# One stream of 53 mixed transfers in place of one key and one value transfer per head, in a decode step with a long cache

## The chip, the cores and the metric

The kernel runs on one core of one Trainium2 chip. Its time is the device time of one execution in microseconds. Before the change three runs gave 1057.06, 1057.39 and 1058.13 us; the median is 1057.39 us. All tensors are float32.

## The reference

One token passes through a block with modulation, attention over a cache of 8192 positions, and a small dense layer.

```python
mod = (_silu(c) @ w_mod)                       # 640 -> 6 x 640: sa, ca, ga, sb, cb, gb
h = _layernorm(x) * (1 + ca) + sa
# attention, 32 heads of 192, 8192 positions, one query
q = (h @ wq).reshape(32, 192)
p = softmax(q @ k_cache.T * 192 ** -0.5)       # per head
x = x + ga * ((p @ v_cache) @ wo)
h = _layernorm(x) * (1 + cb) + sb
r = relu(h @ w1 + b1) ** 2                     # 640 -> 1536
x = x + gb * (r @ w2 + b2)                     # 1536 -> 640
```

The two caches are 201 MB each; with the weights the kernel reads 451.8 MB and writes 2560 bytes.

## The kernel before, in words

**Layout.** A head's keys are one tile of 128 partitions x 64 positions x 192 numbers (6.29 MB), its values another of the same size, in an order that suits the value matmuls. Keys of 30 of the 32 heads carry a piece of weights behind them: behind an even head's keys the `wq` columns of the next pair of heads, behind an odd head's the `wo` rows of the pair before (0.98 MB). All these tiles share three buffers of one size (`slot`, line 54). A load waits until the buffer's last readers are done. All loads go out on SyncE's queue, in program order: first `wm0` (the first two modulation vectors' weights, the first query weights and all small vectors), then K and V of each head in turn, then the remaining weights.

**Per head.** `keys` (line 192) takes the tile in two halves of 32 positions: VectorE multiplies all 32 x 192 products by the query in place (line 201), GpSimd adds the two halves of the rows of the last 14 positions (203), and VectorE sums the rows of the first 18 (204) and the halved rows of the last 14 (205). `softmax` (216) takes the maximum over positions on each partition, then over the partitions through a matmul with the identity and a row maximum (218 to 222), and ScalarE takes the exponential, four copies of each (228), with the sum of each row beside it. `values` (233) multiplies the probabilities with the value tile on PE, 24 products of 512 columns per head, three side by side in strips of 32 rows of the result (240). A float32 product is two instructions on PE, so 48 per head.

**Per pair of heads.** One head later `project` (245) divides by the sums and picks the diagonal of the two heads' results on VectorE (lines 254 and 256), and turns the rows into columns through a matmul (258). `attend` (260) multiplies them with `wo`, summing in one PSUM bank over all pairs. `query` (177) makes the two queries of the next pair.

**The end.** The last head's keys come in four pieces. The `wm1` weights come before and behind the last values: the last pair's `wo` rows with the gate of the attention first, then the shift and scale of the second norm. Then come `w1` in two pieces with the last gate's weights (`gb`) behind, and `w2` in five pieces of 6, 3, 1, 1 and 1 blocks. `gather` (275) spreads the sums over the partitions, `layernorm` (100) follows, then the product with `w1` (343), the square of the positive part, the last gate's product (351), some products whose result nothing reads (355), and the product with `w2` (363). The output goes out at line 368.

**Order.** The program fixes the order of instructions on each engine itself; nothing reorders them. Each engine works through its own list and waits for other engines through semaphores.

## Time and profile before

| | |
|---|---|
| median of three runs | 1057.39 us |
| the profiled execution: span | 1055.5 us |
| data moved by SyncE's queue | 451.83 MB |
| mean rate over the span | 428 GB/s |
| VectorE busy | 831.4 us |
| PE busy (matmuls) | 463.7 us |
| GpSimd busy | 194.8 us |
| ScalarE busy | 33.4 us |
| median time to landing, K with weights (7104 KB) | 27.4 us |
| median time to landing, V (6144 KB) | 22.1 us |

The span reaches from the first to the last instruction of the profiled execution; 1.9 us lie between it and the median of the runs, which are timed without a profile. A row such as `DVE k L201 <- DMA k<-in_kw: 134.4, 28, 7.5` says that line 201 on VectorE (DVE) stood idle for 134.4 us in total, 28 times, 7.5 us at the longest, until a transfer into a key tile had landed. PEld is the weight load of PE, SPq SyncE's queue. In a row of a timeline stand the start, the duration, the engine, the line, the operation, what it writes and reads, the shapes, and how many there are; in brackets the idle time before it. In a row of stretches stand the stretch, its length, the busy us of PE, PEld, DVE, ACT and POOL with their instructions, the granted PE clock, the DMA engines' busy share and their rate.

### The profile page before, as it was taken

Reading aid. Unit: us, or ns where it says so; the run is one execution under the profiler, and the core shown is the slowest. Engines: PE = TensorE matmul, PEld = TensorE weight load, DVE = VectorE, ACT = ScalarE, POOL = GpSimd, SP = SyncE. Lnnn points to the kernel's source line nnn. Section 1 sums busy time; section 2 is a strip of 40 time slices with the busy share of each in tenths; the row PEclk is TensorE's granted clock in tenths of the full one; section 3 lists DMA queues with packets and bytes.
Section 4 is the critical chain, followed back from the end, with each engine's and each line's share of the span. In section 5 each row is a group of like instructions: output and inputs, shape, how many; then the busy total and the mean of one; then the engine's idle time right before and its main releaser. Section 6 shows DMA issues by size and latency. Waiting matters only on the chain.

```text
span 1055.5 us, 5687 instructions
## 1 busy us (share of the span) xinstructions
PE 463.7 (44%) x2356; PEld 155.0 (15%) x2356; DVE 831.4 (79%) x409; ACT 33.4 (3%) x88; POOL 194.8 (18%) x72
## 2 busy tenths in 40 slices
PE   3234443355543345463334534335453335535446
PEld 1101111111111111120111111101111111111113
DVE  2886878978787987878888687997878798789963
ACT  1000000000000000000000000000000000000000
POOL 0211112211212221212221212221221221122110
PEclk9667666766666766666676666666666666767769
DMA  9999999999999999999999999999999999999997
GB/s 403 435 434 428 432 440 427 441 424 437 433 433 428 440 424 441 424 439 427 431 437 437 422 442 430 428 439 426 439 429 433 428 438 433 434 427 432 424 426 310
DMA packets 11410, 452.18 MB, mean 428 GB/s; under 512 B 1269, under 2 KB 1273, under 8 KB 1785
## 3 DMA queue, kind: packets, MB, share of 16 engines
q1 hardware_dynamic: 11384, 451.83, 99.3%
q8 instruction: 18, 0.29, 0.1%
q14 instruction: 8, 0.06, 0.0%
HBM read 451.82 MB, written 0.00 MB: 428 GB/s over the span
## 4 chain that ended last, share of the span: by engine, by line
DMA 42%; DVE 39%; PE 17%; ACT 1%; issue 1%; SPq 0%; DVEq 0%; ACTq 0%
DMA k<-in_kw 36%; DVE k L201 21%; PE ps_o L240 14%; DVE sc L204 12%; DVE sc L205 5%; DMA k<-in_ky 3%; DMA w_t<-in_w 2%; PE ps_mx L220 1%; DMA wm_t<-in_wm 1%; ACT p L228 1%; PE ps_sum L97 1%; PE ps_mod L140 1%; PE ps_q L181 1%; DVE nm L222 0%; DVE mp L218 0%
## 5 line engine op out<-in xcount | busy, mean ns | idle before, releaser
L201 DVE TENSOR_TENSOR k<-k,qb 128x6144 f32<-128x6144 f32 (+1 forms) x66 | 419.7, 6359 | 141.6 <-DMA k<-in_kw 134.4
L203 POOL TENSOR_TENSOR k<-k 128x1344 f32<-128x1344 f32 (+1 forms) x66 | 194.1, 2941 | 820.9 <-DVE k L201 476.1
L240 PE MATMUL ps_o<-v,p 128*32 128x512 f32 x1536 | 290.4, 731 | 17.2 <-ACT p L228 17.2
L204 DVE TENSOR_REDUCE sc<-k 128x18 f32<-128x3456 f32 (+1 forms) x66 | 240.5, 3644 | 4.3
L220 PE MATMUL ps_mx<-ident,mp 128*128 128x128 f32 x64 | 25.5, 501 | 416.2 <-DVE mp L218 416.2
L240 PEld LDWEIGHTS ps_o<-v,p 128*32 128x32 f32 x1536 | 68.4, 131 | 215.4 <-issue 193.1
L267 PE MATMUL att_a<-k,oT 128*32 128x320 f32 x180 | 49.6, 720 | 114.2 <-DVE oT L262 113.1
L205 DVE TENSOR_REDUCE sc<-k 128x14 f32<-128x1344 f32 (+1 forms) x66 | 99.0, 1500 | 0.0
L220 PEld LDWEIGHTS ps_mx<-ident,mp 128*128 128x128 f32 x64 | 16.1, 312 | 442.8 <-DVE mp L218 421.0
L181 PE MATMUL ps_q<-k,hR 128*128 128x384 f32 x150 | 52.3, 496 | 0.0
L228 ACT ACTIVATE p<-sc,nm 128x256 f32<-128x256 f32 x32 | 16.2, 508 | 760.6 <-DVE nm L222 496.9
L267 PEld LDWEIGHTS att_a<-k,oT 128*32 128x32 f32 x180 | 13.7, 161 | 136.7 <-DVE oT L262 116.7
L222 DVE TENSOR_REDUCE nm<-ps_mx 128x1 f32<-128x128 f32 x32 | 9.3, 291 | 28.5 <-PE ps_mx L220 28.5
L181 PEld LDWEIGHTS ps_q<-k,hR 128*128 128x128 f32 x150 | 27.3, 190 | 27.9 <-issue 11.7
L254 DVE SCALAR_TENSOR_TENSOR om<-ps_o,r,mask 96x512 f32<-96x512 f32 x32 | 23.9, 747 | 6.5 <-PE ps_o L240 5.4
L256 DVE TENSOR_REDUCE os<-om 96x64 f32<-96x512 f32 x32 | 21.8, 682 | 1.1
L140 PE MATMUL ps_mod<-wm_t,silu 128*32 128x320 f32 (+1 forms) x120 | 11.7, 550 | 14.6 <-DVE silu L128 14.6
L97 PE MATMUL ps_sum<-sp,ones 128*128 128x2 f32 x32 | 9.4, 364 | 17.2 <-ACT p L228 17.2
L183 ACT ACTIVATE qb<-ps_q 128x384 f32<-128x384 f32 x16 | 7.9, 491 | 195.2 <-PE ps_q L181 195.2
L97 PEld LDWEIGHTS ps_sum<-sp,ones 128*128 128x128 f32 x32 | 8.0, 312 | 21.9 <-ACT p L228 21.9
L145 DVE COPY mods<-ps_mod 128x320 f32<-128x320 f32 (+1 forms) x4 | 1.6, 398 | 10.2 <-PE ps_mod L140 10.2
L76 DVE COPY small<-wm_t 128x27 f32<-128x27 f32 x1 | 0.2, 179 | 11.2 <-DMA wm_t<-in_wm 11.2
(77 smaller groups left out, 90.9 us busy)
## 6 DMA issues: line engine op xcount, KB each, us to landing
k<-in_kw SPq DMA_DIRECT2D x29, 7104.0 KB, 27.4
v<-in_vc SPq DMA_DIRECT2D x32, 6144.0 KB, 22.1
k<-in_ky SPq DMA_DIRECT2D x1, 6144.0 KB, 28.3
k<-in_ky SPq DMA_DIRECT2D x2, 3072.0 KB, 21.5
k<-in_kw SPq DMA_DIRECT2D x3, 1536.0 KB, 15.5
wm_t<-in_wm SPq DMA_DIRECT2D x1, 4173.5 KB, 12.7
wm_t<-in_wm SPq DMA_DIRECT2D x1, 3200.0 KB, 29.3
wm_t<-in_wm SPq DMA_DIRECT2D x1, 2560.0 KB, 18.2
```

Of the source, the lines that this page charges most:

```text
L97: nc.tensor.matmul(ps[:, :n], ones, src, start=True, stop=True)
L140: nc.tensor.matmul(ps[32 * g:32 * (g + 1), :n * DG], e[:, b:b + 1].to_broadcast([P, 32]), wb[:, :, DG * g:DG * (g + 1)], start=(b == 0), s ...
L181: nc.tensor.matmul(ps[:, :PW], hR[:, b], w[:, b], start=(b == 0), stop=(b == KB - 1))
L201: nc.vector.tensor_mul(pr, pr, q[:, None, :].to_broadcast([P, n, DH]))
L203: nc.gpsimd.tensor_add(half, half, pr[:, m:, DH // 2:])
L204: nc.vector.tensor_reduce(s[:, :m], pr[:, :m], axis=AX.X, op=ALU.add)
L205: nc.vector.tensor_reduce(s[:, m:], half, axis=AX.X, op=ALU.add)
L220: nc.tensor.matmul(ps[:, :P], mp.to_broadcast([P, P]), ident, start=True, stop=True)
L228: nc.scalar.activation(p, sc[:, :, None].to_broadcast([P, NPOS, 32 // E]), AF.Exp, bias=nm, accum_out=sp[:, h % 2:h % 2 + 1])
L240: nc.tensor.matmul(ps_t[h][32 * g:32 * (g + 1)], p[:, E * j:E * (j + 1)].rearrange("p e r -> p (e r)"), t[:, j, g], start=(j == 0), stop=( ...
L254: nc.vector.scalar_tensor_tensor(om[:n], ps_t.pop(h)[:n].rearrange("p (d e) -> p d e", e=E), r2[:n, a:a + 1], mask[:n, None, :].to_broadca ...
L267: nc.tensor.matmul(att_a[32 * g:32 * (g + 1), :2 * DG], oT[:, 32 * j:32 * (j + 1)], w[:, j, 2 * DG * g:2 * DG * (g + 1)], start=(i == 0 an ...
```

## The change

K and V are no longer loaded head by head. The whole work is laid out as one array in the order of use and cut into 53 chunks, most of them 84 x 192 columns wide (8.26 MB), again in three buffers. A function `plan` writes down for each chunk how many key positions (of 128 x 192 numbers) and how many value units (8 positions each) it holds, and which piece of weights stands behind them.

- The first chunk is the whole first head's keys. Then most chunks hold 44 key positions and 5 value units; with a `wo` piece (0.98 MB) 34, with a `wq` piece (now 512 columns of `wq`, 1.31 MB, 12 pieces in place of 16) 30, with both 20 or 28. Keys end 40 to 84 positions ahead of the values after each of the chunks up to position 1300; from there on chunks hold a unit of values less until the keys are some 120 positions ahead. So the last two chunks hold values alone (and one `wo` piece). The last chunk is loaded in two pieces.
- Chunk n+3 is asked for at the end of the work on chunk n. Behind the chunks come `wm1` (2 pieces), a tile with the last gate's weights ahead of `w1` (2 pieces: the gate with three blocks, then two blocks) and `w2` (3 pieces of 8, 3 and 1 blocks).
- In each chunk come first the query product, then the values whose probabilities are there, the multiplication of all key positions (split where the head changes), GpSimd's half sums over the last 7/16, the evictions of heads that ended in the chunk before, the row sums, and, where a head's keys end, its maximum and exponential. Values that needed that softmax follow it, then the attention product with `wo`.
- Queries and scores live in rings (`qb`, `sc`) in place of a tile per pair or head; the probabilities get two buffers in place of one.
- The eviction picks the diagonal per head without the division; the division is on the three columns after the turn. Turns and maxima go through a transposing product in place of a product with the identity. The sums over partitions are formed from a copy on ScalarE, a transposing product and a row sum. `attend` puts the first 512 of the 640 outputs on one strip of the result and the rest on the three others.
- At the end the three modulation vectors of `wm1` are one product with `gather` after its third block; the last gate (`gate`) runs ahead of `w1`'s product in two halves of 64 rows, with its result copied by ScalarE; one product over the whole array takes the place of the eight on strips whose result nothing reads.

```diff
-W1_CUT = ((0, 3), (3, 2))
-W2_CUT = ((0, 6), (6, 3), (9, 1), (10, 1), (11, 1))
-WARM = 2
+QC = 512
+NQ = H * DH // QC
+RING = 3 * QC
+SRING = 4 * NPOS
+WQ = KB * QC
+UNIT = E * DH
+SLOT = 84 * DH
+VPC = 5
+LEAD_FROM = 1300
+LEAD = 120
+W1_CUT = (KB * D + 3 * FF, KB * D + KB * FF)
+W2_CUT = (8 * D, 11 * D, 12 * D)
+WM_CUT = (WO + 9 * D, WO + 15 * D)
+WARM = 1
...
+def plan():
+
+    chunks, kp, vp, q, o = [], 0, 0, 1, 0
+    while kp < H * NPOS or vp < H * NPOS // E:
+        room, w = SLOT, []
+        if o < NPAIR - 1 and 2 * (o + 1) * NPOS // E <= vp:
+            w.append(("o", o))
+            o, room = o + 1, room - WO
+        used = (QC * (q - 2) - 1) // DH + 1 if q > 2 else 0
+        if q < NQ and kp >= NPOS * (QC * q // DH) - 3 * NPOS // 2 and kp >= NPOS * used:
+            w.append(("q", q))
+            q, room = q + 1, room - WQ
+        if not chunks:
+            nk, nv = NPOS, 0
+        else:
+            v = VPC - 1 if kp >= LEAD_FROM else VPC
+            nk = min(H * NPOS - kp, (room - v * UNIT) // DH)
+            if kp + nk - E * (vp + v) > LEAD:
+                v += 1
+                nk = min(H * NPOS - kp, (room - v * UNIT) // DH)
+            nv = min(H * NPOS // E - vp, (room - nk * DH) // UNIT)
+            while nv and ((vp + nv - 1) // (NPOS // E) + 1) * NPOS > kp + nk:
+                nv -= 1
+            nk = min(H * NPOS - kp, (room - nv * UNIT) // DH)
+        chunks.append((kp, nk, vp, nv, w))
+        kp, vp = kp + nk, vp + nv
+    assert q == NQ and o == NPAIR - 1
+    return chunks
+
+
+def width(chunk):
+    return chunk[1] * DH + chunk[3] * UNIT + sum(WO if t == "o" else WQ for t, _ in chunk[4])
...
+    def gate(m, w):
+
+        ps = psum.tile([P, 512], F32, tag="q", name=f"ps_mod{m}", bufs=2)
+        for b in range(KB):
+            for k in range(2):
+                nc.tensor.matmul(ps[64 * k:64 * (k + 1), :2 * DG], e[:, b:b + 1].to_broadcast([P, 64]),
+                                 w[:, b, 2 * DG * k:2 * DG * (k + 1)], start=(b == 0), stop=(b == KB - 1))
+        for g in range(G):
+            r = slice(32 * g, 32 * (g + 1))
+            nc.scalar.activation(mods[r, m], ps[r, DG * (g % 2):DG * (g % 2 + 1)], AF.Copy)
+
+    chunk_t = {}
+    start = [sum(width(c) for c in PLAN[:n]) * P for n in range(len(PLAN))]
+
+    def load(n):
+        if n < len(PLAN):
+            chunk_t[n] = slot(f"chunk{n}")
+            m = width(PLAN[n])
+            cuts = (m,) if n + 1 < len(PLAN) else ((PLAN[n][3] + 1) // 2 * UNIT, m)
+            pieces = [(kv[start[n]:start[n] + P * m].rearrange("(p n) -> p n", p=P), cuts)]
+        else:
+            name, src, cuts = (("wm1_t", wm1, WM_CUT), ("w1_t", w1, W1_CUT), ("w2_t", w2, W2_CUT))[n - len(PLAN)]
+            chunk_t[name] = slot(name)
+            n, pieces = name, [(src, cuts)]
+        for src, cuts in pieces:
+            a = 0
+            for b in cuts:
+                nc.sync.dma_start(chunk_t[n][:, a:b], src[:, a:b])
+                a = b
+
+    load(0)
+    load(1)
+    mod(0, 2, wm0_t[:, :KB * 2 * D].rearrange("p (b n) -> p b n", b=KB))
...
-    def query(i, w):
+    qb = const.tile([P, RING], F32, name="qb")
+
+    def query(u, w):
         w = w.rearrange("p (b n) -> p b n", b=KB)
-        ps = psum.tile([P, 512], F32, tag="q", name=f"ps_q{i}", bufs=2)
+        ps = psum.tile([P, 512], F32, tag="q", name=f"ps_q{u}", bufs=2)
         for b in range(KB):
-            nc.tensor.matmul(ps[:, :PW], hR[:, b], w[:, b], start=(b == 0), stop=(b == KB - 1))
-        qb_t[i] = work.tile([P, PW], F32, name=f"qb{i}", tag="qb")
-        nc.scalar.activation(qb_t[i], ps[:, :PW], AF.Copy, scale=DH ** -0.5)
+            nc.tensor.matmul(ps, h1[:, b:b + 1].to_broadcast([P, P]), w[:, b], start=(b == 0), stop=(b == KB - 1))
+        nc.scalar.activation(qb[:, QC * u % RING:QC * u % RING + QC], ps, AF.Copy, scale=DH ** -0.5)
...
+    def multiply(t, first, n):
+
+        a = first
+        while a < first + n:
+            h = a // NPOS
+            b = min(first + n, NPOS * (h + 1))
+            pr = t[:, a - first:b - first]
+            q = qb[:, DH * h % RING:DH * h % RING + DH]
+            nc.vector.tensor_mul(pr, pr, q[:, None, :].to_broadcast([P, b - a, DH]))
+            a = b
+
+    def scores(src, first):
+
+        a, n = first, src.shape[1]
+        while a < first + n:
+            b = min(first + n, (a // SRING + 1) * SRING)
+            nc.vector.tensor_reduce(sc[:, a % SRING:a % SRING + b - a], src[:, a - first:b - first], axis=AX.X, op=ALU.add)
+            a = b
 
     ri_t, ps_t, sum_t = {}, {}, {}
...
-                nc.tensor.matmul(ps_t[h][32 * g:32 * (g + 1)], p[:, E * j:E * (j + 1)].rearrange("p e r -> p (e r)"),
-                                 t[:, j, g], start=(j == 0), stop=(j == n - 1))
+            wide = work.tile([P, 2, ED], F32, tag="wide", name=f"wide{h // 2}", bufs=1)
+            nc.scalar.activation(wide, sp[:, :, None].to_broadcast([P, 2, ED]), AF.Copy)
+            ps = psum.tile([P, 512], F32, tag="sm", name=f"ps_sum{h // 2}", bufs=2)
+            nc.tensor.transpose(ps[:, :P], wide.rearrange("p a d -> p (a d)"), ident)
+            sum_t[h // 2] = ps[:, :P]
+        p_t[h] = p
...
+        if h % 2 == 0:
+            os_t["part"] = work.tile([P, 2, ED], F32, tag="os", name=f"os{h // 2}")
+        os_ = os_t["part"]
+        om = work.tile([P, ED, E], F32, tag="om", name=f"om{h}", bufs=1)
+        nc.vector.tensor_mul(om[:n], ps_t.pop(h)[:n].rearrange("p (d e) -> p d e", e=E),
+                             mask[:n, None, :].to_broadcast([n, ED, E]))
+        nc.vector.tensor_reduce(os_[:n, h % 2], om[:n], axis=AX.X, op=ALU.add)
+        if h % 2:
+            i = h // 2
+            os_t[i] = psum.tile([P, 512], F32, tag="sm", name=f"ps_oT{i}", bufs=2)
+            nc.tensor.transpose(os_t[i][:, :n], os_[:n].rearrange("p a d -> p (a d)"), ident[:n, :n])
+
+    def turn(i):
+        oT = work.tile([P, NV], F32, tag="oT", name=f"oT{i}")
+        nc.vector.tensor_reduce(oT, os_t[i][:, :96].rearrange("p (j r) -> p j r", j=NV), axis=AX.X, op=ALU.add)
+        nc.vector.tensor_scalar(oT, oT, ri_t.pop(i), None, op0=ALU.mult)
+        os_t[i] = oT
 
     def attend(i, w):
...
+        oT = os_t.pop(i)
+        w = w.rearrange("p (j n) -> p j n", j=NV)
+        first, last = i == 0, i == NPAIR - 1
+        oW = work.tile([P, NV, 32], F32, tag="oW", name=f"oW{i}")
+        nc.scalar.activation(oW, oT[:, :, None].to_broadcast([P, NV, 32]), AF.Copy)
+        for j in range(NV):
+            nc.tensor.matmul(att_a[96:, :512], oT[:, j:j + 1].to_broadcast([P, 32]), w[:, j, :512],
+                             start=(first and j == 0), stop=(last and j == NV - 1))
+        nc.tensor.matmul(att_a[:96, :NV * (D - 512)], oW.rearrange("p j r -> p (j r)"), w[:, :, 512:],
+                         start=first, stop=last)
...
+    p_t = {}
+    load(2)
+    to_invert, to_evict = None, []
+    for n, (kp, nk, vp, nv, extra) in enumerate(PLAN):
+        t = chunk_t.pop(n)
+        kt = t[:, :nk * DH].rearrange("p (i d) -> p i d", d=DH) if nk else None
+        vt = t[:, nk * DH:nk * DH + nv * UNIT].rearrange("p (j g n) -> p j g n", g=NV, n=E * ED) if nv else None
+        at = nk * DH + nv * UNIT
+        wo_t = None
+        for what, k in extra:
+            w = t[:, at:at + (WO if what == "o" else WQ)]
+            at += w.shape[1]
+            if what == "q":
+                query(k, w)
+            else:
+                wo_t = (k, w)
+        done = (kp + nk) // NPOS - 1 if nk and (kp + nk) // NPOS > kp // NPOS else None
+        late = [v for v in range(vp, vp + nv) if v // (NPOS // E) not in p_t]
+        for v in range(vp, vp + nv):
+            if v not in late:
+                values(vt[:, v - vp], v)
+        if nk:
+            multiply(kt, kp, nk)
+            m = nk - POOL * nk // 16
+            half = kt[:, m:, :DH // 2]
+            nc.gpsimd.tensor_add(half, half, kt[:, m:, DH // 2:])
+        if to_invert is not None:
+            inverse(to_invert)
+            to_invert = None
+        evicted, to_evict = to_evict, []
+        for h in evicted:
+            evict(h)
+        if nk:
+            scores(kt[:, :m], kp)
+        for h in evicted:
+            if h % 2:
+                turn(h // 2)
+        if nk:
+            scores(half, kp + m)
+        if done is not None:
+            softmax(done)
+            if done % 2:
+                to_invert = done // 2
+        for v in late:
+            values(vt[:, v - vp], v)
+        for v in range(vp, vp + nv):
+            if v % (NPOS // E) == NPOS // E - 1:
+                to_evict.append(v // (NPOS // E))
+        if wo_t is not None:
+            attend(*wo_t)
+        load(n + 3)
+
+    wm1_t, w1_t, w2_t = chunk_t["wm1_t"], chunk_t["w1_t"], chunk_t["w2_t"]
+    gb_t = w1_t[:, :KB * D].rearrange("p (b n) -> p b n", b=KB)
+    w1_t = w1_t[:, KB * D:KB * (FF + D)].rearrange("p (b n) -> p b n", b=KB)
...
-    project(NPAIR - 1)
+    for h in to_evict:
+        evict(h)
+    turn(NPAIR - 1)
     attend(NPAIR - 1, wm1_t[:, :WO])
-    mod_b = mod(3, 2, wm1_t[:, WO + KB * D:WO + KB * 3 * D].rearrange("p (b n) -> p b n", b=KB), (2, 2, 1))
-    next(mod_b)
+    mod(2, 3, wm1_t[:, WO:WO + KB * 3 * D].rearrange("p (b n) -> p b n", b=KB), gather)
...
+    hT2 = columns(layernorm(x1, 32, scale_b, lambda: mods[:, 3], "ln2"), DG, "hT2")
+
+    gate(5, gb_t)
...
-    next(mod(5, 1, gb_t))
     idle = psum.tile([P, 512], F32, tag="sm", name="ps_warm", bufs=2)
     for k in range(WARM):
-        for g in range(G):
-            nc.tensor.matmul(idle[32 * g:32 * (g + 1)], ones[:, :32], w1_t[:, k, :512], start=True, stop=True)
+        nc.tensor.matmul(idle, ones, w1_t[:, k, :512], start=True, stop=True)
```

196 lines of the change are left out of this document (51 added, 145 removed).

## The prediction

> **What bounds the kernel.** I read the page's busy lines and DMA rows first, then the busy time by stretches, then the waits of VectorE and of SyncE's queue, and last the timeline of the end.
>
> ```profile
> span 1055.5 us, 5687 instructions
> PE 463.7 (44%) x2356; PEld 155.0 (15%) x2356; DVE 831.4 (79%) x409; ACT 33.4 (3%) x88; POOL 194.8 (18%) x72
> DMA  9999999999999999999999999999999999999997
> DMA packets 11410, 452.18 MB, mean 428 GB/s; under 512 B 1269, under 2 KB 1273, under 8 KB 1785
> q1 hardware_dynamic: 11384, 451.83, 99.3%
> ```
>
> No compute engine is busy over 79% of the span, while the DMA engines are busy in every slice. The queue of SyncE, q1, carries all the data, 451.83 MB, and its packets fill 99.3% of the time of 16 engines. The next rows are stretches (stretch, its length, busy us of PE, PEld, DVE, ACT, POOL, granted clock, DMA share, GB/s).
>
> ```profile
> 0.00:5.00 5.00, 0.00 (x0) 0.00 (x0) 0.87 (x7) 1.28 (x1) 0.70 (x6) 1.00 0.72 247
> 100.00:200.00 100.00, 39.90 (x188) 12.53 (x190) 83.96 (x39) 2.29 (x7) 19.63 (x7) 0.68 1.00 433
> 800.00:900.00 100.00, 42.67 (x190) 12.92 (x190) 83.55 (x39) 2.29 (x7) 21.18 (x7) 0.65 1.00 432
> 1042.00:1044.00 2.00, 2.00 (x17) 0.81 (x13) 0.00 (x0) 0.00 (x0) 0.00 (x0) 0.50 0.96 403
> 1046.00:1048.00 2.00, 2.00 (x33) 1.02 (x28) 1.64 (x5) 0.00 (x0) 0.00 (x0) 1.00 0.79 316
> 1048.00:1050.00 2.00, 1.98 (x60) 1.63 (x55) 0.00 (x0) 0.00 (x0) 0.00 (x0) 1.00 0.56 209
> 1050.00:1052.00 2.00, 1.38 (x36) 0.50 (x27) 0.00 (x0) 0.00 (x0) 0.00 (x0) 1.00 0.08 31
> ```
>
> In the eight hundreds of microseconds from 100 to 900 (first and last shown) the share is 1.00 and the rate 432 to 433 GB/s. So the stream never starves there, and only three things can move the time: the start (the first 5 us run at 247 GB/s), the cost of a byte and of a packet in the stream, and what follows the last byte. At the end the share falls over 6 us: the 16 engines do not finish together.
>
> ```profile
> DVE k L201 <- DMA k<-in_kw: 134.4, 28, 7.5
> SPq L155 <- DVE sc L205: 567.6, 29, 23.7
> ```
>
> VectorE waits for K 28 times; SyncE's queue waits for buffers, but the 1.00 share says a transfer is always left in flight meanwhile. A faster or slower engine in the middle therefore changes nothing until the queue runs dry.
>
> **The change, part one: the stream.** Working the new plan through, it is 53 chunks, nearly all 16128 or 16000 columns (8.26 or 8.19 MB, rows of about 64 KB in place of 57 and 49 KB), and the bytes are the same. Transfers: 1 for the first weights, 52 whole chunks, the last chunk in 2, then 2, 2 and 3 for the weights behind it: 62 loads in place of 79. Each load is 128 rows and 16 semaphore writes, 144 packets: 79 x 144 + 8 for the output is the 11384 of the page, and 62 x 144 + 8 = 8936. So 2448 packets go, 153 on each engine. What one costs comes from two stretches, 200 to 900 us and 1030 to 1052 us, the second full of short rows (packets, MB, share):
>
> ```profile
> q1 hardware_dynamic: 6411, 302.72, 100.1%
> ...
> q1 hardware_dynamic: 1057, 7.78, 84.8%
> ```
>
> 700 us x 16 x 1.001 = 11211 engine-us and 22 x 16 x 0.848 = 298.5. With one price per MB and one per packet, the pair of equations gives 11.6 ns a packet. The saving is 153 x 11.6 ns = 1.8 us. Ends: nothing, if the price is of bytes alone; and 2.4 us from the stretch 1048 to 1050, where 209 GB/s at 0.56 is 373 at full share in 2560-byte rows against 433, which is 16 ns a packet. I take 1.8, from the longer stretches. The Trainium skill, "DMA: Bandwidth & Descriptors", section "Anatomy of one DMA", fits about 2 us fixed plus bytes per transfer on another issue path; taken as serial that would make 17 loads fewer worth 34 us. The trace speaks against it: the stream is 100% busy between 200 and 900 us, so a fixed cost lies under the next transfer.
>
> **Part two: does the stream stay full?** Transfer n+3 goes out when chunk n has been used by all engines, so after chunk n lands there are two more, 2 x 19.1 us, in the queue (8.26 MB at 433 GB/s).
>
> ```profile
> L201 DVE TENSOR_TENSOR k<-k,qb 128x6144 f32<-128x6144 f32 x62 | 406.3, 6553 | 141.6 <-DMA k<-in_kw 134.4 <-ACT qb L183 4.4 <-DMA k<-in_ky 2.8
> L204 DVE TENSOR_REDUCE sc<-k 128x18 f32<-128x3456 f32 x62 | 232.7, 3753 | 4.1
> L205 DVE TENSOR_REDUCE sc<-k 128x14 f32<-128x1344 f32 x62 | 95.7, 1543 | 0.0
> L254 DVE SCALAR_TENSOR_TENSOR om<-ps_o,r,mask 96x512 f32<-96x512 f32 x32 | 23.9, 747 | 6.5 <-PE ps_o L240 5.4
> L256 DVE TENSOR_REDUCE os<-om 96x64 f32<-96x512 f32 x32 | 21.8, 682 | 1.1
> L218 DVE TENSOR_REDUCE mp<-sc 128x1 f32<-128x64 f32 x32 | 7.0, 220 | 1.1
> L222 DVE TENSOR_REDUCE nm<-ps_mx 128x1 f32<-128x128 f32 x32 | 9.3, 291 | 28.5 <-PE ps_mx L220 28.5
> ```
>
> A key position costs VectorE (6553 + 3753 + 1543) / 32 = 370 ns. A head adds 747 + 682 for the eviction, 220 + 291 and a 0.9 us wait (28.5 / 32) for the maximum, and an estimated 0.45 us for the new small steps (row sums, inverse, scale), together 3.3 us. The mean chunk has 2048 / 51 = 40 positions: 14.9 + 2.1 = 17.0 us of the 19.1; the largest, 60, takes 25.5 us against 38 until the queue is dry. Splits at head ends and the ring add some 40 short instructions to VectorE, ScalarE (3% busy) gets two small copies a pair, POOL's half-adds keep their share of the positions, and PE (44%) loses passes: queries 160 to 120, attention rows 204 to 128. All of it lies under that slack and is costed at nothing; with the slack gone each us would count in full. The new waits: the attention matmuls of a pair stand behind the chunk's maximum on PE's queue, and the chunk's refill and the next chunk's query and value matmuls stand behind them; both have the 13 us that are left. Keys running 120 ahead of values make the last value units ready when they land, so their matmuls do not wait for a softmax.
>
> The tightest refill is the fourth chunk.
>
> ```profile
> 24.75 6.25 PE L181 MATMUL ps_q<-wm_t,hR 128*128 128x384 f32 x10 [1.93 <-DVE hR L175]
> 23.88 0.82 DVE L175 COPY hR<-ln_h 128x640 f32<-128x640 f32 x1
> 31.04 0.49 ACT L183 ACTIVATE qb<-ps_q 128x384 f32<-128x384 f32 x1 [7.92 <-PE ps_q L181]
> 31.56 6.56 DVE L201 TENSOR_TENSOR k<-k,qb 128x6144 f32<-128x6144 f32 x1 [4.44 <-ACT qb L183]
> ```
>
> The first load grows by 0.33 MB (0.8 us), the hR copy (0.8 us) goes, and the query of 512 columns takes 6.25 x 512 / 384 = 8.3 us; with ScalarE's 0.6 for 512 columns VectorE starts near 33.7 us in place of 31.6. 64 positions at 370 ns end at 57.4, and the fourth chunk goes out. Bytes ahead of it (4.60 + 6.29 + 8.19 + 8.26 MB at 433, plus 2.1 us for the slow first 5) last until 65.2: 7.8 us to spare. Start: 0.
>
> **Part three: the end.** T is the landing of the last weight piece.
>
> ```profile
> 1022.71 7.50 PE L240 MATMUL ps_o<-v,p 128*32 128x512 f32 x48
> 1039.47 5.13 PE L343 MATMUL ps_f<-w_t,hT 128*32 128x384 f32 x40 [2.10 <-issue]
> 1040.11 0.16 PEld L343 LDWEIGHTS ps_f<-w_t,hT 128*32 128x32 f32 x4 [0.17 <-issue]
> 1040.43 0.16 PEld L343 LDWEIGHTS ps_f<-w_t,hT 128*32 128x32 f32 x4 [0.17 <-issue]
> 1041.44 0.27 PEld L343 LDWEIGHTS ps_f<-w_t,hT 128*32 128x32 f32 x4 [0.37 <-issue]
> 1042.08 0.27 PEld L343 LDWEIGHTS ps_f<-w_t,hT 128*32 128x32 f32 x4 [0.37 <-issue]
> 1044.38 1.57 PE L140 MATMUL ps_mod<-w_t,silu 128*32 128x160 f32 x40
> 1044.65 0.56 DVE L346 TENSOR_TENSOR f<-ps_f,bbt 128x384 f32<-128x384 f32 x1 [5.29 <-PE ps_f L343]
> 1046.23 0.58 DVE L82 STREAM_TRANSPOSE fT<-f 128x384 f32<-128x384 f32 x1
> 1047.46 3.16 PE L363 MATMUL ps_y<-w_t,fT 128*32 128x160 f32 x80
> 1049.32 0.97 PEld L363 LDWEIGHTS ps_y<-w_t,fT 128*32 128x32 f32 x32 [0.34 <-DMA w_t<-in_w]
> 1051.71 0.48 PE L363 MATMUL ps_y<-w_t,fT 128*32 128x160 f32 x8 [0.31 <-DMA w_t<-in_w]
> ```
>
> Before, w2's matmuls already wait for bytes (1049.32, 1051.71): the end hangs on T = 1051.7, and 3.8 us follow, which the change leaves as they are. After it, 15.4 MB lie behind the last V piece, 35.6 us at 433. Going back from T by their bytes, the pieces land at: w2's 8 blocks T-3.1, w1's second piece T-9.1, the gate with three w1 blocks T-12.8, the rest of wm1 T-22. Before that stand the last 3 value units (18 / 48 of 7.50 us), the eviction, the last attention rows and three modulation vectors; the layer norm's row sums are then done ahead of T-12.8, so the gate starts there. It has 20 passes of 320 columns, two side by side; 40 of 160, four side by side, took 1.57 us, so 10 pairs take 3.1: T-9.7. w1: a set of four takes 0.32 us at full clock (1040.11 to 1040.43), ten sets 3.2: T-6.5. The four VectorE steps (1044.65 to 1046.81): T-4.3, 1.2 us ahead of w2. So the cover of the gate moved forward is 1.2 us, where before it ran behind w1 for nothing. At half clock a set takes 0.64 (1041.44 to 1042.08). If the gate's first 3.4 us run so, as long as it lasted here (about 1040.8 to 1044.1), 1.7 us are lost and the chain is 0.5 us late; 5 us cost 1.3. I take +0.3 us, as most of this lies in the cover. Ends: 0, and +2.5 where w2's first blocks (some 2.2 us) also run slow.
>
> The Trainium skill, "TensorE: Matmul & The Clock Gate", section "What's actually happening", has the clock halved after an idle window of about 3.4 us. The trace agrees on the halving (0.50 in 1042 to 1044), after only 2.1 us of idleness.
>
> **The sum.** -1.8 + 0 + 0 + 0.3 = -1.5 us: a span of 1054.0. The profiled span lies 1.9 us under the median of the runs; carried over, 1057.4 - 1.5 = **1055.9 us**. About 0.2%, 2.1 us, is what a measurement tells from no change, so this is the same, at its faster edge.
>
> **Rivals.** *The engines finish closer together.* The shares 0.79, 0.56 and 0.08 leave 2 x (0.21 + 0.44 + 0.92) = 3.1 us of idle engine time ahead of T. Equal, larger transfers and fewer short pieces could halve it: another -1.6, 1054.3 us. For it: the price of a packet can also reach 2.4. Against: the lag may come from elsewhere, such as instruction loads.
> *The packets cost nothing that counts*: then 1057.4 to 1057.7.
> *The end becomes PE's.* No row shows a gate on 64-column halves. If its halves do not run side by side, it takes 6.2 us in place of 3.1; with 1.7 us of half clock the chain is 3.1 + 1.7 - 1.2 = 3.6 late, and with w2's first blocks slow too 5.8: 1057.4 - 1.8 + 3.6 = 1059.2 to 1061.4, slower. It decides from about 3.9 us on, when it outweighs the saving by 2.1. For it: the half clock at 1042 in the same place; against: before, groups did run side by side.
> *VectorE becomes the stream's bound*: its 17.0 us a chunk would have to grow by over 12%; at 15%, 51 x 0.5 = 25 us, 1082. Against: its instructions are the same ones, only regrouped.
>
> **Chances.** The forecast 0.32 and no gain 0.10: same 0.42. Finishing together or dearer packets: faster 0.39. PE's end 0.14, VectorE 0.05: slower 0.19. The range: 2.4 plus 1.6 at the low end gives 1053.4; at the high end no saving and a slow clock, 1057.4 + 2.2 = 1059.6, leave out two in ten. The forecast case's own range is 1055.3 to 1057.
>
> **What would show it.** Right: about 8936 packets in q1, 433 to 434 GB/s from 100 to 900 us, PE's last w2 matmul waiting for DMA near 1050. Wrong: a slice with a DMA share under 9 in the middle (a dry queue), or a last w2 matmul that waits for fT (PE's end). The range fails if the stream stops in the middle.

## The result, and the profile after

The changed kernel takes 1055.99 us (median of 20 runs, 1055.27 to 1057.15), the kernel before on the same chips 1057.80 us (20 runs, 1057.06 to 1058.17). The ratio is 0.9986, with an interval of 0.9979 to 0.9992: 1.8 us faster, or 0.14%. The forecast was 1055.9 us with a gain of 1.5 us, "the same, at its faster edge"; the gain is inside the 0.2% that was named there as what a measurement can tell from no change, and the interval excludes none at all. The profiled execution has a span of 1053.8 us, against 1055.5 us before.

The page of the changed kernel, its first lines and its DMA rows:

```profile
span 1053.8 us, 5121 instructions
PE 495.8 (47%) x2102; PEld 134.6 (13%) x2102; DVE 830.2 (79%) x428; ACT 43.4 (4%) x122; POOL 188.1 (18%) x57
...
DMA  9999999999999999999999999999999999999997
...
q1 hardware_dynamic: 8936, 451.83, 99.3%
```

SyncE's queue has 8936 packets, as worked out from the plan. The DMA engines are busy in every slice, and VectorE is busy for 830 us against 831. PE runs fewer instructions (2102 in place of 2356) and is busy for longer, 495.8 us against 463.7; the prediction spoke of passes that PE loses and not of this, but at 47% of the span PE is not what bounds the kernel.

The stretches of the changed kernel (stretch, length, busy us of PE, PEld, DVE, ACT, POOL, granted clock, DMA share, GB/s):

```profile
100.00:900.00 800.00, 376.24 (x1448) 97.92 (x1448) 659.78 (x312) 28.76 (x87) 151.72 (x43) 0.70 1.00 433
1036.00:1038.00 2.00, 1.59 (x8) 0.92 (x10) 1.26 (x5) 0.26 (x1) 0.00 (x0) 0.60 1.02 426
1038.00:1040.00 2.00, 2.00 (x12) 0.88 (x10) 0.10 (x1) 0.00 (x0) 0.00 (x0) 0.55 1.11 475
1044.00:1046.00 2.00, 1.55 (x10) 0.30 (x2) 1.36 (x3) 0.00 (x0) 0.00 (x0) 1.00 0.81 335
1046.00:1048.00 2.00, 1.02 (x32) 1.05 (x36) 1.22 (x4) 0.00 (x0) 0.00 (x0) 1.00 0.53 219
1048.00:1050.00 2.00, 2.00 (x66) 2.00 (x61) 0.00 (x0) 0.00 (x0) 0.00 (x0) 1.00 0.17 61
```

From 100 to 900 us the share stays 1.00: the plan with three buffers never lets the queue run dry. The last three stretches are the fall at the end, 0.81, 0.53 and 0.17, in place of 0.79, 0.56 and 0.08: the same slope, two microseconds earlier. In 1036 to 1040 PE's clock is 0.60 and 0.55.

The timeline of the end of the changed kernel (start, duration, engine, line, operation, out<-in, shapes, count; in brackets the idle time before):

```profile
998.95 0.22 DVE L271 TENSOR_REDUCE mp<-sc 128x1 f32<-128x64 f32 x1
...
1015.88 6.21 PE L298 MATMUL ps_o<-chunk,p 128*32 128x512 f32 x42
1024.59 2.76 PE L331 MATMUL att_a<-wm_t,oT 128*32 128x512 f32 x6 [0.68 <-DVE oT L321]
1036.71 4.43 PE L188 MATMUL ps_mod<-w_t,silu 128*64 128x320 f32 x20 [0.41 <-DMA w_t<-in_w]
1041.07 3.43 PE L428 MATMUL ps_f<-w_t,hT 128*32 128x384 f32 x40
1046.14 0.58 DVE L122 STREAM_TRANSPOSE fT<-f 128x384 f32<-128x384 f32 x1
1046.98 3.47 PE L446 MATMUL ps_y<-w_t,fT 128*32 128x160 f32 x96 [1.43 <-DVE gb L440]
1050.51 0.33 DVE L449 TENSOR_TENSOR y<-ps_y,mods 128x160 f32<-128x160 f32 x1 [3.22 <-PE ps_y L446]
```

The last softmax (`mp`) stands at 999, the last values and the last attention rows follow it, and the gate (`ps_mod`, line 188) begins when its weights land, after a wait of only 0.41 us. `ps_y`, the product with `w2`, waits for no bytes: VectorE ends its wait of 1.43 us. Before, the last `w2` matmul began at 1051.71; now `ps_y` ends at 1050.45, so the end moved forward with the span.

### The profile page after: what moved, and what is told of

Read it like the earlier page. It is cut to its first block, busy times and chain, and to the rows that moved or that the text cites. A ratio compares the mean times of both kernels' runs of the same rounds, so it can differ in the third digit from the quotient of the medians.

```text
span 1053.8 us, 5121 instructions
## 1 busy us (share of the span) xinstructions
PE 495.8 (47%) x2102; PEld 134.6 (13%) x2102; DVE 830.2 (79%) x428; ACT 43.4 (4%) x122; POOL 188.1 (18%) x57
## 3 DMA queue, kind: packets, MB, share of 16 engines
q1 hardware_dynamic: 8936, 451.83, 99.3%
## 4 chain that ended last, share of the span: by engine, by line
DMA 56%; DVE 31%; PE 11%; ACT 1%; issue 0%; SPq 0%; DVEq 0%
DMA chunk<-in_kv 53%; DVE chunk L249 16%; DVE sc L257 13%; PE ps_o L298 5%; DMA w_t<-in_w 2%; PE ps_q L230 2%; PE att_a L331 2%; DMA wm_t<-in_wm 1%; DVE os L312 1%; DVE om L310 1%; ACT p L281 0%; PE ps_mod L179 0%; PE ps_mx L273 0%; PE ps_mod L188 0%; PE att_a L333 0%
## 5 line engine op out<-in xcount | busy, mean ns | idle before, releaser
L249 DVE TENSOR_TENSOR chunk<-chunk,qb 128x8064 f32<-128x8064 f32 (+19 forms) x81 | 419.7, 5211 | 128.4 <-DMA chunk<-in_kv 123.2
L257 DVE TENSOR_REDUCE sc<-chunk 128x25 f32<-128x4800 f32 (+21 forms) x109 | 333.9, 3097 | 0.4
L298 PE MATMUL ps_o<-chunk,p 128*32 128x512 f32 x1536 | 296.7, 736 | 73.7 <-DMA chunk<-in_kv 64.3
L376 POOL TENSOR_TENSOR chunk<-chunk 128x1824 f32<-128x1824 f32 (+9 forms) x51 | 187.4, 3674 | 806.3 <-DVE chunk L249 548.4
L298 PEld LDWEIGHTS ps_o<-chunk,p 128*32 128x32 f32 x1536 | 67.4, 131 | 278.1 <-issue 188.1
L331 PE MATMUL att_a<-chunk,oT 128*32 128x512 f32 x90 | 63.4, 863 | 42.2 <-DVE oT L321 42.2
L230 PE MATMUL ps_q<-chunk,ln_h 128*128 128x512 f32 x110 | 66.9, 769 | 26.1 <-DMA chunk<-in_kv 26.1
L230 PEld LDWEIGHTS ps_q<-chunk,ln_h 128*128 128x128 f32 x110 | 26.5, 252 | 64.5 <-issue 35.1
L310 DVE TENSOR_TENSOR om<-ps_o,mask 96x512 f32<-96x512 f32 x32 | 21.6, 675 | 8.5 <-PE ps_o L298 8.5
L320 DVE TENSOR_REDUCE oT<-ps_oT 128x3 f32<-128x96 f32 x16 | 4.0, 248 | 20.3 <-PE ps_oT L316 20.3
L333 PE MATMUL att_a<-chunk,oW 128*96 128x384 f32 x30 | 14.1, 550 | 0.0
## 6 DMA issues: line engine op xcount, KB each, us to landing
w_t<-in_w SPq DMA_DIRECT2D x1, 3904.0 KB, 20.7
```

The costliest lines, as they stand in the source:

```text
L230: nc.tensor.matmul(ps, h1[:, b:b + 1].to_broadcast([P, P]), w[:, b], start=(b == 0), stop=(b == KB - 1))
L249: nc.vector.tensor_mul(pr, pr, q[:, None, :].to_broadcast([P, b - a, DH]))
L257: nc.vector.tensor_reduce(sc[:, a % SRING:a % SRING + b - a], src[:, a - first:b - first], axis=AX.X, op=ALU.add)
L298: nc.tensor.matmul(ps_t[h][32 * g:32 * (g + 1)], p[:, E * j:E * (j + 1)].rearrange("p e r -> p (e r)"), t[:, g], start=(j == 0), stop=last)
L310: nc.vector.tensor_mul(om[:n], ps_t.pop(h)[:n].rearrange("p (d e) -> p d e", e=E), mask[:n, None, :].to_broadcast([n, ED, E]))
L331: nc.tensor.matmul(att_a[96:, :512], oT[:, j:j + 1].to_broadcast([P, 32]), w[:, j, :512], start=(first and j == 0), stop=(last and j == NV ...
```

## The experiments

Each kernel is the changed one with one edit or two, but for the second, which edits the kernel before. The kernel before ran beside each and took 1057.65 to 1057.77 us; "more than the change" compares with the 1055.99 us above. The interval of each ratio is about 2 us wide, so differences of 1 us or less between two of these kernels are read from the rows and not from the medians. Each profile shows one execution, and where the same bytes land differs between executions by some tenths of a microsecond up to 1 us.

**What does a packet cost? Chunks in two column halves.** The same bytes, 52 more loads, 7488 more packets (468 on each engine).

```diff
-            cuts = (m,) if n + 1 < len(PLAN) else ((PLAN[n][3] + 1) // 2 * UNIT, m)
+            cuts = (m // 2, m) if n + 1 < len(PLAN) else ((PLAN[n][3] + 1) // 2 * UNIT, m)
```

> The changed kernel with chunks 0 to 51 loaded in two column halves each: 52 loads more, each engine gets 52 x 9 = 468 packets more, and the rows are 32 KB in place of 64 KB. If the saving is the price of packets (11.6 ns each), this costs 468 x 11.6 ns = 5.4 us against the changed kernel and ends about 3.6 us over the kernel before (ratio 1.0035); at 16 ns a packet 7.5 us. If packets cost nothing and the gain came from the end or from the engines finishing closer together, it stays at the changed kernel's time, 1.8 us under the kernel before.

It took 1060.47 us (6 runs, 1059.65 to 1061.12), 4.5 us more than the change; against the kernel before the ratio is 1.0028 (1.0016 to 1.0039). The DMA view of 200 to 900 us counts SyncE's packets, the MB they moved and the share. First the changed kernel:

```profile
q1 hardware_dynamic: 5282, 302.88, 100.0%
```

Then the kernel with halves:

```profile
q1 hardware_dynamic: 10538, 301.62, 100.2%
```

Both queues are full for the whole 700 us, and the one with 328 more packets on each engine (5256 / 16) moved 1.26 MB less, which at 433 GB/s is 2.9 us: 8.9 ns a packet. From the total, 4.5 us / 468 gives 9.6. So a packet has a price of its own, though less than the 11.6 ns of the prediction.

**The same question in the kernel before.** Each value tile in two loads: 32 more loads, 4608 more packets (288 on each engine).

```diff
-CUTS = {("k", H - 2): 2, ("k", H - 1): 4}
+CUTS = {("k", H - 2): 2, ("k", H - 1): 4} | {("v", h): 2 for h in range(H)}
```

> The kernel before with every head's values loaded in two column halves: 32 loads and 32 x 9 = 288 packets per engine more. At 11.6 ns a packet +3.3 us over the kernel before (ratio 1.0032). If the price of packets holds only for the new kernel, or is nothing, no change.

It took 1060.29 us (10 runs, 1059.81 to 1060.42), 2.5 us more than the kernel before; ratio 1.0024 (1.0014 to 1.0033). That is 8.8 ns a packet. Its timeline shows that the end still hangs on the bytes:

```profile
1054.27 0.48 PE L363 MATMUL ps_y<-w_t,fT 128*32 128x160 f32 x8 [0.32 <-DMA w_t<-in_w]
```

The row's partner in the kernel before began at 1051.71, also behind a wait for DMA; it is 2.56 us later, 8.9 ns a packet. This is the cleanest of the prices, as nothing but the landing of bytes sets it, in one execution of each kernel.

**Packets or loads?** One load of 16 rows of 4 bytes behind each of 52 chunks: 52 more loads as in the first experiment, but 104 more packets on each engine in place of 468.

```diff
+    tiny = const.tile([16, len(PLAN) - 1], F32, name="tiny")
...
         load(n + 3)
+        if n + 1 < len(PLAN):
+            nc.sync.dma_start(tiny[:, n:n + 1], wm0[:16, n:n + 1])
```

> The changed kernel with one more load of 16 rows of 4 bytes behind each of the first 52 chunks: 52 loads more, on each engine one row and one semaphore packet, 104 packets. The two-piece loads cost 4.5 us for 52 loads and 468 packets. If that was a price of packets (some 9 ns each), this costs about 1 us and ends 0.9 us under the kernel before; if it was a price of loads (86 ns each), it costs 4.5 us again and ends 2.7 us over it.

It took 1057.66 us (10 runs, 1057.09 to 1058.76), 1.7 us more than the change; ratio to the kernel before 1.0002 (0.9993 to 1.0011). Its page counts the packets:

```profile
span 1055.3 us, 5175 instructions
...
q1 hardware_dynamic: 10600, 451.83, 99.3%
```

A load costs 1.7 / 52 = 32 ns here and 4.5 / 52 = 86 ns where it has 144 packets. If loads had the price, both would be the same. With the price on packets, it is 16 ns here, or 14 by the spans (1055.3 against 1053.8), and 9 to 10 there. So the price follows packets more than loads, without being one constant.

**Chunks in two halves of 64 partitions.** The same bytes and the same number of loads as with column halves, but each row stays whole.

```diff
-                nc.sync.dma_start(chunk_t[n][:, a:b], src[:, a:b])
+                for r in (slice(0, 64), slice(64, P)) if n in range(len(PLAN) - 1) else (slice(0, P),):
+                    nc.sync.dma_start(chunk_t[n][r, a:b], src[r, a:b])
```

> The changed kernel with chunks 0 to 51 loaded in two halves of 64 partitions each: 52 loads more, but the same rows of 64 KB, so each engine gets only 52 semaphore packets more. If the price is one of packets (rows and semaphores alike), this costs 52 x 11.6 ns = 0.6 us, and the time is 1.2 us under the kernel before. If the price is one of loads (1.8 us / 17 loads = 0.1 us each), it costs 5.4 us, as the column halves do, and ends 3.6 us over the kernel before.

It took 2124.92 us (4 runs, 2117.86 to 2126.82), a ratio of 2.0071 (2.0032 to 2.011). The row of SyncE's queue on its page,

```profile
q1 hardware_dynamic: 9768, 451.83, 99.7%
```

and a stretch of the same kernel:

```profile
800.00:900.00 100.00, 27.41 (x100) 6.13 (x100) 48.86 (x24) 1.79 (x6) 11.11 (x3) 0.59 1.01 209
```

There are only 832 more packets (9768 - 8936), and the DMA share is full, yet the rate is 209 GB/s in place of 433. As a price of packets this run says nothing; it shows that a load over half the partitions runs at half the rate while its engines look busy. The Trainium skill, "SBUF — State Buffer", section "Door 1: The DMA port swizzle", says that the rate depends on how many of 16 ports the partitions of a transfer reach, and its map gives 64 partitions in a row 8 of the 16; the 209 against 433 agrees with it.

**Has VectorE slack to spare?** Five more row sums of 286 ns, which change nothing, in each chunk.

```diff
             evict(h)
+        for _ in range(5):
+            nc.vector.tensor_reduce(mask, ident.rearrange("p (g e c) -> p e g c", g=G, e=E), axis=AX.XY, op=ALU.add)
```

> The changed kernel with five repeats of a small row sum on VectorE (286 ns each, the same result written again) in every chunk: 1.4 us more on VectorE per chunk, 17.0 to 18.4 of the 19.1 us that a chunk's transfer takes. If the middle is bound by the stream, with two chunks in the queue, nothing happens: the changed kernel's time, 1.8 us under the kernel before. If VectorE sits close to the bound (chunks of 44 positions come to some 20 us), the queue runs dry in places and it costs 5 us or more.

It took 1058.22 us (10 runs, 1057.22 to 1058.81), 2.2 us more than the change; ratio 1.0005 (0.9995 to 1.0014). I had expected nothing. A stretch of it:

```profile
800.00:900.00 100.00, 46.88 (x190) 12.12 (x184) 86.89 (x70) 3.30 (x10) 20.12 (x6) 0.74 1.00 432
```

The timeline of its end:

```profile
983.29 8.56 DVE L249 TENSOR_TENSOR chunk<-chunk,qb 128x8064 f32<-128x8064 f32 x1
1001.39 0.22 DVE L271 TENSOR_REDUCE mp<-sc 128x1 f32<-128x64 f32 x1
1038.65 4.53 PE L188 MATMUL ps_mod<-w_t,silu 128*64 128x320 f32 x20
```

The stream is still full in the middle (1.00, 432 GB/s). At the end the last softmax is 2.44 us later than in the changed kernel, and the gate begins 1.94 us later. 2.44 less the 0.41 us that the gate waited for its weights before is 2.03, so the lateness of the softmax would do for the loss. But the bytes are as late: the gate's weights are asked for at 1018.28 and land 20.3 us after that, at 1038.6, in place of 1015.98 + 20.7 = 1036.7. Chain and weights arrive together, and this execution does not show which of the two cost the 2.2 us.

**The same, in the first 40 chunks only.**

```diff
+        for _ in range(5 if n < 40 else 0):
```

> The changed kernel with the five repeats of a small row sum on VectorE in the first 40 chunks only. If the 2.2 us that the repeats cost in every chunk came from the last chunks, where the last softmax starts the end's chain, nothing is left: the changed kernel's time, 1.8 us under the kernel before. If they came from the middle, most of the 2.2 us stays and it is level with the kernel before.

It took 1056.73 us (10 runs, 1056.17 to 1057.40), 0.7 us more than the change; ratio 0.9993 (0.9984 to 1.0002). Its timeline:

```profile
983.28 8.56 DVE L249 TENSOR_TENSOR chunk<-chunk,qb 128x8064 f32<-128x8064 f32 x1 [1.35 <-DMA chunk<-in_kv]
999.91 0.22 DVE L271 TENSOR_REDUCE mp<-sc 128x1 f32<-128x64 f32 x1
1037.70 4.42 PE L188 MATMUL ps_mod<-w_t,silu 128*64 128x320 f32 x20 [0.43 <-DMA w_t<-in_w]
```

The gate waits for its weights again, and two thirds of the 2.2 us are gone, although 40 of the 53 chunks keep their 57 us of extra work (40 x 5 x 0.286). In the middle VectorE's slack is real. The work on the last chunk with keys begins at the same time as with sums in every chunk (983.28 and 983.29), so of the 2.44 us there 1.48 are the five sums of that one chunk (1001.39 - 999.91), and the other 0.96 are bytes that land later. They fit the 0.7 us that stay here: the gate's weights land some 1 us later than in the changed kernel, though the last 13 chunks have no sums. Why they are later the runs do not show. The pages count 7 `q14 instruction` packets for the changed kernel, 8 here and 9 with sums in every chunk, so more loads of instructions are a possible cause; but the run with two filling products further below has 7, and its gate's weights land 0.7 us later too.

**What is the lead at the end for?** The chunks behind position 1300 keep five value units.

```diff
-LEAD_FROM = 1300
+LEAD_FROM = 9999
```

> The changed kernel without the growing lead of the keys at the end: chunks keep five value units, and the last head's keys end in the last chunk but one. The last softmax then comes some 13 us later, about 34 us before the last byte, and its eight value units after it. By the working back from the last byte the attention rows start about 2.5 us later and w1's product some 1 us later: 0 to 1.5 us slower than the changed kernel. If the lead carries the gain, 5 us or more slower, and slower than the kernel before.

Its runs are 1058.87, 1058.88, and four from 1061.93 to 1062.61, with a median of 1062.21 us; ratio 1.0031 (1.0019 to 1.0043). It is 3 to 6 us slower than the change, more than I had expected. The timeline of a run of 1058.87 us:

```profile
1014.02 0.22 DVE L271 TENSOR_REDUCE mp<-sc 128x1 f32<-128x64 f32 x1
1029.95 2.76 PE L331 MATMUL att_a<-wm_t,oT 128*32 128x512 f32 x6 [0.61 <-DVE oT L321]
1041.53 2.91 PE L188 MATMUL ps_mod<-w_t,silu 128*64 128x320 f32 x20
1050.29 3.47 PE L446 MATMUL ps_y<-w_t,fT 128*32 128x160 f32 x96 [1.43 <-DVE gb L440]
```

The last softmax is 15 us later (1014.02), the last attention rows 5.4 us, and the gate 4.8 us, behind no wait for DMA, though it now runs at full clock (2.91 us). `ps_y` begins 3.3 us later. The end has become PE's and VectorE's: the rival that ends on the slower side, reached by another road than the one it was given.

**Does the gate's place ahead of `w1` cost anything?** The gate's weights and its product go behind `w1`'s, as in the kernel before.

```diff
-W1_CUT = (KB * D + 3 * FF, KB * D + KB * FF)
+W1_CUT = (3 * FF, KB * D + KB * FF)
...
-    gb_t = w1_t[:, :KB * D].rearrange("p (b n) -> p b n", b=KB)
-    w1_t = w1_t[:, KB * D:KB * (FF + D)].rearrange("p (b n) -> p b n", b=KB)
+    gb_t = w1_t[:, KB * FF:KB * (FF + D)].rearrange("p (b n) -> p b n", b=KB)
+    w1_t = w1_t[:, :KB * FF].rearrange("p (b n) -> p b n", b=KB)
...
-    gate(5, gb_t)
     pf = psum.tile([P, 512], F32, tag="q", name="ps_f", bufs=2)
...
+    gate(5, gb_t)
     idle = psum.tile([P, 512], F32, tag="sm", name="ps_warm", bufs=2)
...
-        "w1": np.concatenate([rows(wm[:, 5 * D:], KB), rows(B_w1, KB)], axis=1),
+        "w1": np.concatenate([rows(B_w1, KB), rows(wm[:, 5 * D:], KB)], axis=1),
```

> The changed kernel with the last gate's weights behind w1 again (two loads as before: three w1 blocks, then two blocks and the gate) and its product behind w1's product. If the end of the changed kernel hangs on PE's chain, some 0.5 us behind the bytes, w2's product starts earlier, waits for its bytes, and 0.5 us go (about 2.3 us under the kernel before). If the end hangs on the bytes anyway, no change (1.8 us under). If the gate ahead of w1 was worth something, 1 to 2 us slower.

It took 1057.32 us (11 runs, 1056.46 to 1058.08), 1.3 us more than the change; ratio 0.9995 (0.9986 to 1.0003). I had expected a small gain. Its timeline:

```profile
1038.28 5.92 PE L427 MATMUL ps_f<-w_t,hT 128*32 128x384 f32 x40 [1.85 <-DVE hT L122]
1044.13 2.91 PE L188 MATMUL ps_mod<-w_t,silu 128*64 128x320 f32 x20
1045.85 0.58 DVE L122 STREAM_TRANSPOSE fT<-f 128x384 f32<-128x384 f32 x1
1046.97 1.12 PE L438 MATMUL ps_warm<-w_t,ones 128*128 128x512 f32 x2
1048.03 3.47 PE L446 MATMUL ps_y<-w_t,fT 128*32 128x160 f32 x96
```

Now `w1`'s product is the one that runs at half clock, 5.92 us against 3.43; the gate and the product behind it then keep PE for 3.9 us, more than the four VectorE steps beside them take (2.2 us, from the end of `w1`'s product, 1038.28 + 5.92, to that of `fT`, 1045.85 + 0.58), and `ps_y` waits in PE's queue. Ahead of `w1` the gate meets the slow clock itself, and most of what that costs lies in time that waits for bytes. So against this arrangement the gate's place is worth about 1 us in the profiled executions (`ps_y` begins at 1048.03 in place of 1046.98).

**Can the slow clock be avoided?** Two products whose result nothing reads, after the three modulation vectors.

```diff
+    busy = psum.tile([P, 512], F32, tag="sm", name="ps_busy", bufs=2)
+    for k in range(2):
+        nc.tensor.matmul(busy, ones, wm1_t[:, 512 * k:512 * (k + 1)], start=True, stop=True)
```

> The changed kernel with two products of 128 x 512 whose result nothing reads, on PE right behind the three modulation vectors, in the 1.9 us in which PE waits for the layer norm's first sum. If the half clock in the gate is what makes PE's chain late, the gate takes 3.1 us in place of 4.4, w2's product starts 1.3 us earlier and waits for its bytes: 0.5 us less than the changed kernel. If the clock does not matter there, or the end hangs on the bytes, no change.

It took 1056.69 us (11 runs, 1055.42 to 1057.22); ratio 0.9987 (0.9979 to 0.9996). Its timeline:

```profile
1033.23 1.99 PE L415 MATMUL ps_busy<-wm_t,ones 128*128 128x512 f32 x4
...
1037.43 4.60 PE L188 MATMUL ps_mod<-w_t,silu 128*64 128x320 f32 x20 [0.42 <-DMA w_t<-in_w]
```

The gate took 4.60 us, so the clock fell nevertheless, and the run says nothing on what the slow clock costs. The same edit together with the gate behind `w1`:

> Both edits together. If the end then hangs on the bytes, it is as fast as the better of the two alone, 0.5 us under the changed kernel, and not their sum. If each edit shortens the path by itself, 1 us under.

This took 1056.88 us (11 runs, 1055.55 to 1057.85); ratio 0.9991 (0.9982 to 0.9999). Its timeline:

```profile
1038.71 6.03 PE L430 MATMUL ps_f<-w_t,hT 128*32 128x384 f32 x40 [1.85 <-DVE hT L122]
```

`w1`'s product stayed at half clock, 6.03 us, so it is as little of a test.

**Three such products,** one of them between the two sums of the second norm.

```diff
-    def layernorm(x, copies, scale1, shift, name):
+    def layernorm(x, copies, scale1, shift, name, after_sum=lambda: None):
...
         tm = total(s, name + "_tm")
+        after_sum()
...
+    fill(2)
...
-    hT2 = columns(layernorm(x1, 32, scale_b, lambda: mods[:, 3], "ln2"), DG, "hT2")
+    hT2 = columns(layernorm(x1, 32, scale_b, lambda: mods[:, 3], "ln2", lambda: fill(1)), DG, "hT2")
```

> The changed kernel with three products whose result nothing reads: two behind the modulation vectors, as before, and one more between the layer norm's two sums, so that PE is busy for most of the 4 us ahead of the gate. If the half clock in the gate follows from idleness there, the gate takes 2.9 us in place of 4.4, w2's product starts 1.5 us earlier and waits for bytes: 0.4 us less than the changed kernel, too little for the clock, but visible in the rows. If the clock falls at a fixed time after the values, the gate still takes 4.4 us.

It took 1056.85 us (11 runs, five from 1055.37 to 1055.83 and six from 1056.85 to 1057.34); ratio 0.9989 (0.998 to 0.9998). The profiled execution is of the first group, with a span of 1053.8 us. Its timeline:

```profile
1033.10 1.98 PE L418 MATMUL ps_busy<-wm_t,ones 128*128 128x512 f32 x4
...
1035.33 1.10 PE L418 MATMUL ps_busy<-wm_t,ones 128*128 128x512 f32 x2
...
1037.03 2.91 PE L189 MATMUL ps_mod<-w_t,silu 128*64 128x320 f32 x20 [0.16 <-DMA w_t<-in_w]
1044.95 0.58 DVE L122 STREAM_TRANSPOSE fT<-f 128x384 f32<-128x384 f32 x1
1046.93 3.52 PE L454 MATMUL ps_y<-w_t,fT 128*32 128x160 f32 x96 [2.57 <-DMA w_t<-in_w]
1050.52 0.33 DVE L457 TENSOR_TENSOR y<-ps_y,mods 128x160 f32<-128x160 f32 x1 [4.42 <-PE ps_y L454]
```

The gate takes 2.91 us in place of 4.43, and `fT` is 1.2 us earlier. `ps_y` now waits for DMA and begins at 1046.93, 0.05 us from where it began with the slow clock. That does not make the slow clock free, as the bytes of this execution are later: the gate begins when its weights land in both, here at 1037.03, in the changed kernel at 1036.71, 0.32 us earlier. The first piece of `w2` shows the same. It is asked for at 1021.07 here and lands 25.7 us after that, at 1046.8; in the changed kernel at 1022.14 and 24.3 us after that, at 1046.4. With its own bytes the changed kernel could have begun `ps_y` near 1046.6, and began at 1046.98. So of the 1.5 us that the gate loses, 0.3 to 0.4 us reach the end; the rest is covered by the wait for bytes.

Whether the three products kept the clock up is not shown. Here the slow stretch came earlier, on the last attention rows (`att_a`, 4.33 us from 1023.51 on, in place of 2.76), ahead of the first of these products. The run with the tiny loads has none of them; its attention rows took 4.15 us, and its gate ran as fast:

```profile
1038.98 2.91 PE L188 MATMUL ps_mod<-w_t,silu 128*64 128x320 f32 x20
```

**The same, with `w2` in five pieces** as in the kernel before, so that fewer products lie behind the last landing.

```diff
-W2_CUT = (8 * D, 11 * D, 12 * D)
+W2_CUT = (6 * D, 9 * D, 10 * D, 11 * D, 12 * D)
```

> The three filling products, and w2 in the five pieces of the kernel before (6, 3, 1, 1 and 1 blocks) in place of three. With the filling alone the gate ran at full clock, the chain came 1.5 us earlier, and w2's product then waited for its first piece: the end was the same to the hundredth. If it hangs on that first piece of 8 blocks and 3.5 us of products behind it, the smaller pieces let the product start earlier and end 1.0 us behind the last byte, as in the kernel before: 0.2 to 0.4 us less, minus 0.2 us for two loads more. If the end hangs on the last byte anyway, nothing. Either way less than 0.5 us, shown by the rows and not by the clock.

It took 1055.61 us (11 runs, 1055.37 to 1056.44); ratio 0.9982 (0.9973 to 0.9991). Its timeline:

```profile
1046.44 3.19 PE L454 MATMUL ps_y<-w_t,fT 128*32 128x160 f32 x88 [1.43 <-DVE gb L448]
1049.90 0.48 PE L454 MATMUL ps_y<-w_t,fT 128*32 128x160 f32 x8 [0.26 <-DMA w_t<-in_w]
1050.45 0.33 DVE L457 TENSOR_TENSOR y<-ps_y,mods 128x160 f32<-128x160 f32 x1 [3.70 <-PE ps_y L454]
```

Now the last products wait for the last bytes, with nothing else in their way, and `y` is written at 1050.45, 0.06 us earlier than in the changed kernel, although the last bytes land 0.3 us later here: at 1049.9, where the last product begins, against 1022.99 + 26.6 = 1049.6 there. This is the end that the bytes allow. The median is the lowest of all, but its interval overlaps that of the change (0.9979 to 0.9992) for the most part, so I do not call it faster than the change.

## Why the prediction was right

**The stream's price: right in kind, too large by 0.4 us.** The 153 packets on each engine were to save 1.8 us at 11.6 ns. The runs put a packet of a long stream at 8.8 and 9.6 ns by the medians and at 8.9 by the stretch of 200 to 900 us, so the term is 153 x 8.9 = 1.4 us. The 11.6 came from a pair of equations whose second stretch, the last 22 us, holds short rows only, at a time when the engines finish one after another. In the run with the tiny loads, with rows of 4 bytes, a packet cost 14 to 16 ns, so one price for both stretches probably mixed two; no run has the price of the end's own rows. The upper end of the prediction, 16 ns, is 15 by the rows that it names (2560 bytes at 373 and at 433 GB/s over 16 engines).

**The start: 0, as forecast.** VectorE was to begin near 33.7 us, and the fourth chunk to be asked for at 57.4. The timeline of the changed kernel:

```profile
24.09 7.21 PE L230 MATMUL ps_q<-wm_t,ln_h 128*128 128x512 f32 x10 [1.08 <-DVE ln_h L159]
31.97 12.96 DVE L249 TENSOR_TENSOR chunk<-chunk,qb 128x12288 f32<-128x12288 f32 x1 [5.17 <-ACT qb L231]
```

The timeline of SyncE's queue alone:

```profile
1.20 54.33 SPq L210 DMA_DIRECT2D chunk<-in_kv  x4
```

The query took 7.21 us where 8.3 were forecast, VectorE began at 31.97, and the fourth load was out by 55.5 (1.20 + 54.33), with the stream full behind it.

**The middle: 0, as forecast, but its argument does not reach to the end.** VectorE's slack was put at 2 of 19.1 us a chunk; it is busy for 659.78 of 800 us, 82%, so 3.4 us a chunk are free. The waits of the changed kernel for the same two lines as before:

```profile
DVE chunk L249 <- DMA chunk<-in_kv: 123.2, 42, 8.9
SPq L210 <- DVE sc L257: 752.5, 50, 24.9
```

VectorE waits for a landing 42 times, and SyncE's queue waits for buffers while the share stays full. The sentence that each us on VectorE counts only once the slack is gone does not hold for the last chunks: there the last softmax starts the chain to the gate, which has 0.4 us to spare. Without the extra lead the kernel loses 3 to 6 us by that road. The 2.2 us of five short sums a chunk are not parted in this way: 1.5 us of sums in one chunk and bytes that landed later came together. The prediction named the lead for the values alone, and had the row sums of the second norm done ahead of T-12.8 without going back further than the values. In the trace the last values end near 1022.1 (1015.88 + 6.21) and the chain arrives at the gate 0.4 us before its weights. It was right there by little.

**The end: +0.3 forecast, 0.3 to 0.4 measured, in one execution.** The mechanism came as told. With T, the landing of the last piece, at 1049.6, the gate's weights land 12.9 us ahead of it and the first piece of `w2` 3.2 us (12.8 and 3.1 forecast). The gate starts when its weights land, its two halves run side by side (2.91 us at full clock; 3.1 forecast), the clock is at about half at its beginning, and the gate loses 1.5 us (4.43 - 2.91; 1.7 forecast). The cover was put at 1.2 us, and `ps_y` begins 0.3 to 0.4 us after its bytes would have let it. One of the prediction's own signs misled: a last `w2` product that waits for VectorE and not for DMA was to show that it was wrong, and that is what the changed kernel has. But a chain that is 0.3 us late, as its sum had it, already means this.

**The sum.** The terms as measured are -1.4 + 0 + 0 + 0.3 to 0.4, about -1.0, and the runs give -1.8 with an interval of -2.2 to -0.8 (from the ratio). The profiled executions say where the rest is: the last piece lands 2.1 us earlier (1049.6 in place of 1051.7), 0.7 us more than the packets' price, and what follows it takes 4.2 us in place of 3.8. The 0.7 us are given to no cause. The same stream lands that much later in another execution (the gate's weights at 1036.71 in the changed kernel and at 1037.43 with two filling products). The page also counts 16 `q8 instruction` packets in place of 18; that fewer loads of instructions brought the landing forward is a rival that no run tested. The forecast of -1.5 came from a price too large by 0.4 us and left out these 0.7 us, so part of the agreement is luck. Another part: the three runs shown had a median of 1057.39 us, 20 runs have 1057.80.

**The rivals.** *Engines finishing closer together* is hardly seen: the idle engine time in the last three stretches is 2 x (0.19 + 0.47 + 0.83) = 3.0 us against 3.1, of which 0.4 and 0.3 us lie behind the last landing, so at most some 0.2 us came from there in these two executions. *Packets cost nothing* fell by three runs (column halves, the kernel before with halved values, the tiny loads). *PE's end* did not come at its price, as the halves of the gate run side by side; the trial without the lead shows that such an end is near, and with 3 to 6 us it costs what the rival had said (1.8 to 4.0 slower than before; that trial was 1.1 to 4.8 slower). *VectorE as the stream's bound* did not come: even with five sums more the share stays 1.00.
